# A fused attention, gated layer and routed experts: a re-costed order, an affine tie mask, single blocks for ScalarE, transposes pair by pair

## Chip, cores and metric

The kernel runs on one core of one Trainium2 chip. The metric is device microseconds of one execution; the profile has, beside it, the span from the first to the last instruction of the program.

## What is computed

Three stages follow one another: causal linear attention with decay over 2 x 8 heads of 768 positions; a layer `x @ w_in`, gated by `clip(h + 3, 0, 6) / 6`, and `@ w_out`; and a routed layer of eight experts, in which each of 1536 tokens goes to one expert and each expert takes at most 192. The third, cut:

```python
logits = x @ w_gate
order = np.argsort(-logits.flatten())
assigned, counts = -np.ones(N), np.zeros(E)
for idx in order:                       # best (token, expert) pairs first
    tok, e = int(idx) // E, int(idx) % E
    if assigned[tok] >= 0 or counts[e] >= cap:
        continue
    assigned[tok] = e
    counts[e] += 1
out = np.zeros((N, D))
for e in range(E):
    mask = assigned == e
    out[mask] = np.maximum(x[mask] @ w1[e], 0.0) @ w2[e]
```

## The kernel before

**Who sets the order.** The program is written as steps, each with an engine, a cost in us, inputs, buffers and a key. `Plan.run` (lines 95 to 160) simulates them by these numbers and emits the instructions in the order in which its simulation starts them. It picks, of the steps that could start about now on an engine, the one with the lowest key. On the chip each engine then takes its instructions in that order and waits only for real data and real buffers. So a wrong cost does not break anything; it puts instructions into another order. A PE step that depends on another engine is planned 0.16 (`LAT`) plus 0.4 (`SLACK`, line 55) after its input. Steps of SP, which issues DMAs, mostly cost 0.06 in the plan.

**Pools.** `B` has 21 buffers of 8 KB a partition, `H` 2, `Q` 11; a step that needs a buffer waits until one is free.

**Stages.** (1) Attention over twelve chunks of 128 positions (`attention`), conversion of the weights into pairs of fp16 (`weights`, `split`), and h = x @ w_in with the gate (`h_unit`). Each product is three fp16 matmuls (high by high, high by low, low by high). (2) x2 = g @ w_out (`x2_part`, lines 677 to 715), twelve blocks j of 128 tokens, 768 matmuls in all, for the last four blocks in two parts of 384 and 128 columns. In the same stretch runs the routing.

**Routing** (lines 779 to 858) takes seven phases, one after the other. In each, m holds a value per token; PE spreads it over all partitions (L787), ACT copies it to `mrow` (L789), and for each of twelve blocks i a mask G of 128 x 1536 tells which tokens come before: DVE makes blocks 0 to 7 (L816, L825), ACT makes the lower part of blocks 8 to 11 in two steps (sign, L819; step, L822), and PE counts (L838). Ties are masks `eq` per block: POOL compares blocks 0 to 5 (L795) and multiplies all six by `before`, a triangular mask, in one instruction (L797); DVE does blocks 6 to 11 in one instruction each (L801). When all counts are in, DVE makes F (L848), PE flags, DVE the next m (L762). After the last phase pos tells each token's row.

**From routing to experts.** POOL scatters xsa (three quarters of x2) and xsb (the rest and the token numbers) to DRAM, twelve scatters each (L886), issued one after the other. SP reads them back transposed for each pair of experts (L906, L907: xs), and loads row numbers (L912) and the experts' weights (L984).

**Experts.** Eight experts in four pairs. `layer1` (L931): hp = xs @ w1, a first part over xsa and a second over xsb; ACT applies relu (rr, L936); the high part of h goes to DVE (L400) and the low part to POOL (L402). `layer2` (L960): po = h @ w2, then ACT (os) and a scatter to the output. Weights come as 32 loads of 1 MB; ACT makes the high halves (L398, L393), DVE most low halves (L408).

## Time and profile before

| | us |
|---|---|
| median of 3 runs | 569.48 (568.6 to 569.69) |
| the profiled execution | 569.23 |
| its span | 567.5 |
| PE busy | 508.1 (90%) |
| DVE busy | 423.2 (75%) |
| POOL busy | 314.2 (55%) |
| ACT busy | 294.3 (52%) |

The page gives busy time per engine, a chain of work that ended last, and groups of instructions by line. A timeline merges an engine's instructions of one kind into one row: the start, the time from the first one's start to the last one's end, and in brackets the engine's idle time before them with what ended it. An instruction that is held by something it shares with another engine shows as a longer duration and not as a wait.

### The profile page before, as it was taken

The numbers are of one execution on the slowest core, as the hardware profiler recorded it, in microseconds if no ns is written. First come the engines' busy times: TensorE is split into PE (matmuls) and PEld (weight loads), VectorE is DVE, ScalarE is ACT, GpSimd is POOL, SyncE is SP. The second block draws the span as 40 slices with busy tenths as digits, with TensorE's granted clock in tenths as the row PEclk, the third lists the DMA queues.
The fourth block names the chain that finished last, engine by engine and source line by source line (L and its number), as shares of the span: only waits on it lengthen the run. The fifth ranks groups of instructions, "written<-read, shape, count | busy, mean of one in ns | idle before, by whom it ended". The sixth has DMA issues, their size and how long they took to land.

```text
span 567.5 us, 10531 instructions
## 1 busy us (share of the span) xinstructions
PE 508.1 (90%) x4293; PEld 312.1 (55%) x4295; DVE 423.2 (75%) x651; ACT 294.3 (52%) x379; POOL 314.2 (55%) x279
## 2 busy tenths in 40 slices
PE   6889789898999878999999999999556599999995
PEld 3667444587786334444444344546556268676772
DVE  6799997787989893698696897897440669989410
ACT  2137664445454545383683684585330568787510
POOL 3887596746734645164052363254882458868531
PEclk9799989898999998999999999999968799999998
DMA  7996091380148427000000003206735999995001
GB/s 231 417 413 166 19 295 58 83 253 33 43 186 183 109 43 113 1 2 1 1 1 2 1 2 117 106 9 243 274 106 83 316 383 411 348 316 243 27 20 55
DMA packets 47889, 81.02 MB, mean 143 GB/s; under 512 B 33753, under 2 KB 34785, under 8 KB 41697
## 3 DMA queue, kind: packets, MB, share of 16 engines
q1 hardware_dynamic: 45728, 73.97, 40.9%
q0 software_dynamic: 2112, 6.39, 2.9%
q8 instruction: 33, 0.54, 0.4%
q14 instruction: 16, 0.12, 0.1%
HBM read 66.61 MB, written 6.40 MB: 129 GB/s over the span
## 4 chain that ended last, share of the span: by engine, by line
PE 50%; DVE 22%; POOL 9%; issue 8%; DMA 7%; ACT 3%; SPq 0%; POOLq 0%; ACTq 0%; DVEq 0%
PE x2p L686 17%; PE hp L931 9%; PE po L960 9%; PE cp L838 3%; POOL xsa L886 3%; POOL xsb L886 2%; DVE r L576 2%; DVE G L825 2%; PE xo L541 2%; DVE wod L381 2%; PE xo L538 2%; PE h L216 1%; PE h L217 1%; DMA raw<-raw 1%; DVE wid L381 1%
## 5 line engine op out<-in xcount | busy, mean ns | idle before, releaser
L686 PE MATMUL x2p<-wo,g 128*128 128x512 f16 (+2 forms) x768 | 139.3, 327 | 2.2 <-DVE xa L701 2.0
L402 POOL TENSOR_TENSOR g<-r,g 128x512 f16<-128x512 f32 (+1 forms) x52 | 74.7, 1444 | 63.5 <-ACT g L398 63.4
L216 PE MATMUL h<-xT,wi 128*128 128x256 f16 (+2 forms) x304 | 90.4, 308 | 6.8 <-DVE r L576 6.8
L408 DVE SCALAR_TENSOR_TENSOR w<-ws,w 128x1024 f16<-128x1024 f32 x58 | 79.0, 1403 | 20.1 <-ACT w L398 20.0
L686 PEld LDWEIGHTS <-g 128*128 128x128 f16 x768 | 62.0, 98 | 57.4 <-issue 15.3
L795 POOL TENSOR_SCALAR eq<-mrow,m 128x128 bf16<-128x128 f32 x42 | 45.9, 1109 | 82.0 <-ACT mrow L789 82.0
L217 PE MATMUL h<-xT,wi 128*128 128x256 f16 (+2 forms) x304 | 90.1, 307 | 0.5 <-DVE xT L546 0.5
L218 PE MATMUL h<-xT,wi 128*128 128x256 f16 (+2 forms) x304 | 89.9, 306 | 0.0
L931 PE MATMUL hp<-xs,w 128*128 128x192 f16 x768 | 68.3, 252 | 16.3 <-DMA xs<-xsa 11.4
L931 PEld LDWEIGHTS <-w 128*128 128x128 f16 x768 | 65.7, 100 | 20.3 <-issue 18.7
L398 ACT ACTIVATE w<-ws 128x1024 f16<-128x1024 f32 x64 | 64.3, 1050 | 15.8 <-DMA ws<-w 11.2
L960 PE MATMUL po<-w,h 128*64 128x512 f16 (+1 forms) x384 | 65.8, 385 | 6.5 <-ACT rr L936 6.5
L402 POOL TENSOR_TENSOR h<-rr,h 128x384 f16<-128x384 f32 x32 | 44.5, 1396 | 36.4 <-DVE h L400 36.3
L398 ACT ACTIVATE g<-r 128x512 f16<-128x512 f32 (+1 forms) x52 | 30.5, 592 | 45.4 <-DVE r L576 45.4
L825 DVE TENSOR_SCALAR G<-mrow,m 128x1408 bf16<-128x1408 f32 (+10 forms) x77 | 52.8, 715 | 0.8 <-issue 0.8
L960 PEld LDWEIGHTS <-h 128*64 128x64 f16 (+1 forms) x384 | 29.4, 105 | 39.5 <-issue 10.0
L575 ACT ACTIVATE r<-h,c 128x512 f32<-128x512 f32 (+1 forms) x52 | 33.5, 646 | 28.9 <-PE h L218 20.2
L400 DVE TENSOR_SCALAR h<-rr 128x384 f16<-128x384 f32 x32 | 22.6, 719 | 32.3 <-ACT rr L936 32.2
L576 DVE SCALAR_TENSOR_TENSOR r<-r,h 128x512 f32<-128x512 f32 (+1 forms) x52 | 32.8, 639 | 18.2 <-ACT r L575 17.5
L819 ACT ACTIVATE G<-mrow,m 128x1536 bf16<-128x1536 f32 (+3 forms) x28 | 39.3, 1404 | 3.0 <-PE cp L838 1.7
L217 PEld LDWEIGHTS <-wi 128*128 128x128 f16 x304 | 30.2, 99 | 19.0 <-issue 7.3
L216 PEld LDWEIGHTS <-wi 128*128 128x128 f16 x304 | 30.2, 99 | 17.8 <-DVE r L576 2.8
(169 smaller groups left out, 810.9 us busy)
## 6 DMA issues: line engine op xcount, KB each, us to landing
ws<-w SPq DMA_DIRECT2D x32, 1024.0 KB, 7.4
wis<-w_in SPq DMA_DIRECT2D x8, 1024.0 KB, 14.3
wos<-w_out SPq DMA_DIRECT2D x8, 1024.0 KB, 5.9
raw<-raw SPq DMA_DIRECT2D x12, 512.0 KB, 11.8
qk<-raw SPq DMA_DIRECT2D x48, 128.0 KB, 5.1
vk<-raw SPq DMA_DIRECT2D x6, 512.0 KB, 4.4
tab<-tz SPq DMA_DIRECT2D x1, 512.0 KB, 6.3
wt<-wo SPq DMA_TRANSPOSE x16, 3.4
```

The costliest lines, as they stand in the source:

```text
L216: te.matmul(ps, lh, rh, start=start, stop=False)
L217: te.matmul(ps, lh, rl, start=False, stop=False)
L218: te.matmul(ps, ll, rh, start=False, stop=stop)
L398: h = add("se", c_se(n), lambda: se.activation(dst()[0], src(), AF.Copy, scale=sc), deps, bufs, key, reserve)
L402: lo = add("ge", c_ge(n), lambda: ge.tensor_tensor(dst()[1], src(), dst()[0], op=OP.subtract), [h], bufs, key)
L408: lo = add("ve", c_ve(n), lambda: ve.scalar_tensor_tensor(dst()[1], src(), sc, dst()[0], op0=OP.mult, op1=OP.subtract), [h], bufs, key)
L576: t = add("ve", c_ve(nf * T), lambda: ve.scalar_tensor_tensor(r[:], r[:], 6.0 * 2.0 ** -11, ps[:], op0=OP.min, op1=OP.mult), [t], [ps, r], ...
L686: te.matmul(ps[:], gsl(y, fc, j), w[:, z, fc % 4, d0:d1], start=(fc + y + z == 0), stop=(fc == 15 and y == 1))
L795: t_eq.append(add("ge", 1.06, lambda i=i, eq=eq, mrow=mrow: ge.tensor_scalar(eq[:, i], mrow[:, P * i:P * i + P], m[:, i:i + 1], None, op0= ...
L825: ve.tensor_scalar(G[:, i % 2, o:], mrow[:, o:], m[:, i:i + 1], None, op0=OP.is_le)
L931: te.matmul(ps[:, i], w[:, z, kk % 2, cl], x[:, 2 * kk + y, CAP * i0:CAP * i0 + CAP], start=(i + kk + y + z == 0), stop=(i == 1 and kk == ...
L960: te.matmul(o, h1[e][:, y, k, cl], w2[e, fh][0][:, zz, f], start=(k + y + zz == 0), stop=(k == 7 and y == 1))
```

## The change

- The plan's costs are set anew: SP steps (0.06 becomes 0.34 to 0.45 for loads, 2.3 for the four loads of a q or k part, 1.4 for a transpose of w_out, 1.25 to 4.7 for one of xs, 2.5 for the rows), the compares of DVE, the two steps of ACT, POOL's scatters and others. PE steps of the routing (keys below -1e5) get a fifth of the slack, 0.08.
- POOL's product with `before` becomes an affine selection on the same 128 x 768 elements: it keeps an element where its column is greater than its partition and writes 0 elsewhere. The ties lie in two buffers of pool Q rather than one of H.
- G of blocks 8 to 11 lies in one-block buffers of pool H rather than in pairs in B; blocks 0 to 7 stay in pairs in B.
- The transposes of pairs 1 to 3 depend, in the plan, on the first layer 1 matmuls of the pair before; in the old kernel those of xsa came after pair 0's xsb, and those of xsb after the scatters alone.
- The low part of h is made by DVE (the same line's other branch, L408) rather than by POOL.

```diff
+    URGENT = -1e5
-            t = max(t, end + (self.SAME[e] if x == e else self.LAT + self.SLACK[e]))
+            t = max(t, end + (self.SAME[e] if x == e else self.LAT + (self.SLACK[e] if s.key > self.URGENT else 0.2 * self.SLACK[e])))
...
 def c_cmp(n):
-    return 0.12 + n * 0.00058
-def c_cmp_se(n):
-    return 0.1 + n * 0.00095
+    return 0.11 + n * 0.00056
+def c_sign(n):
+    return 0.04 + n * 0.00099
+def c_step(n):
+    return 0.2 + n * 0.00073
...
-        return [add("sp", 0.06, lambda z=z: sy.dma_start(b[:, z * n:(z + 1) * n], raw_d[c, :, z * n:(z + 1) * n]),
+        return [add("sp", 0.45 if c > 3 else 0.06, lambda z=z: sy.dma_start(b[:, z * n:(z + 1) * n], raw_d[c, :, z * n:(z + 1) * n]),
...
-            ld_q = [add("sp", 0.24, lambda part=part: load(part), after, [qk], RAW_KEY[c], 0, 1 << 19) for part in (1, 0)]
+            ld_q = [add("sp", 2.3, lambda part=part: load(part), after, [qk], RAW_KEY[c], 0, 1 << 19) for part in (1, 0)]
...
-        eq = buf("H", [P, NCH, P], BF, f"eq{p}")
+        eqs = [buf("Q", [P, 6, P], BF, f"eq{p}_{i}") for i in range(2)]
...
-        t_eq = [add("ge", 0.26 * BY_GE, lambda eq=eq: ge.tensor_tensor(
-            eq[:, 0:BY_GE], eq[:, 0:BY_GE], before.unsqueeze(1).to_broadcast([P, BY_GE, P]), op=OP.mult), t_eq, [eq], GK)]
+        t_eq = [add("ge", 1.3, lambda eq=eqs[0]: ge.affine_select(
+            out=eq[:], in_=eq[:], pattern=[[0, BY_GE], [1, P]], compare_op=OP.is_gt, fill=0.0, base=0,
+            channel_multiplier=-1), t_eq, [eqs[0]], GK)]
...
-        Gs = [buf("B", [P, 2, NCH * P], BF, f"G{p}_{i}") for i in range(NCH // 2)]
+        Gs = [buf("B", [P, 2, NCH * P], BF, f"G{p}_{i}") for i in range(BY_SE // 2)]
+        Gs += [buf("H", [P, 1, NCH * P], BF, f"G{p}_{i}") for i in range(BY_SE, NCH)]
...
-                t = [add("se", c_cmp_se(o), sgn, t_row[:i // 4 + 1], [G, mrow], GK + n)]
-                t = [add("se", c_cmp_se(o), step, t, [G], GK + n)]
+                t = [add("se", c_sign(o), sgn, t_row[:i // 4 + 1], [G, mrow], GK + n)]
+                t = [add("se", c_step(o), step, t, [G], GK + n)]
...
-        first = t_xs[0][1:] if q else []
-        t_xs[q] = [add("sp", 0.06, lambda: sy.dma_start_transpose(out=xs[q][:, 0:6], in_=xsa_d[r, :]), t_sa + first, [xs[q]], key, 0, 725000),
-                   add("sp", 0.06, lambda: sy.dma_start_transpose(out=xs[q][:, 6:8], in_=xsb_d[r, 0:256]), t_sb, [xs[q]], key, 0, 242000)]
+        first = [l1_first[2 * q - 2]] if q else []
+        t_xs[q] = [add("sp", 4.7 if q else 2.4, lambda: sy.dma_start_transpose(out=xs[q][:, 0:6], in_=xsa_d[r, :]), t_sa + first, [xs[q]], key, 0, 725000),
+                   add("sp", 1.25, lambda: sy.dma_start_transpose(out=xs[q][:, 6:8], in_=xsb_d[r, 0:256]), t_sb + first, [xs[q]], key, 0, 242000)]
...
             t_h1[e] += split(lambda r=r: r[:], lambda u=u: (h1[e][:, 0, 2 * u:2 * u + 2], h1[e][:, 1, 2 * u:2 * u + 2]),
-                             384, 1.0, "ge", [t], [r, h1[e]], key - 50, "ve")
+                             384, 1.0, "ve", [t], [r, h1[e]], key - 50, "ve")
...
-    for q in range(NE // 2):
-        experts_in(q, f_key + 34 * q - 20 if q else -1e6)
-    t_rows = add("sp", 0.3, load_rows, t_sb, [], f_key, 0, 500000)
+    experts_in(0, -1e6)
+    t_rows = add("sp", 2.5, load_rows, t_sb, [], f_key, 0, 500000)
...
-                ld = add("sp", 0.06, lambda e=e, z=z, n=n, st=st, src=src: sy.dma_start(st[:], src[e, :, z * n:(z + 1) * n]),
+                ld = add("sp", 0.4, lambda e=e, z=z, n=n, st=st, src=src: sy.dma_start(st[:], src[e, :, z * n:(z + 1) * n]),
...
     for q in range(NE // 2):
+        if q:
+            experts_in(q, f_key + 34 * q - 20)
         for e in (2 * q, 2 * q + 1):
```

## Rows read from the trace of the kernel before

**Rows 1.** Stretches: bounds, length, busy (instructions) PE PEld DVE ACT POOL, clock, DMA, GB/s

```profile
0.00:236.40 236.40, 208.32 (x1795) 133.60 (x1798) 194.83 (x236) 112.14 (x163) 145.67 (x118) 0.95 0.53 159
236.40:391.00 154.60, 154.14 (x1146) 71.34 (x1144) 128.09 (x322) 97.68 (x103) 59.69 (x52) 1.00 0.12 40
391.00:417.75 26.75, 13.35 (x209) 12.17 (x206) 18.39 (x21) 11.36 (x16) 23.57 (x33) 0.87 0.62 210
417.75:448.40 30.65, 19.22 (x192) 18.42 (x192) 5.83 (x8) 5.98 (x11) 12.04 (x18) 0.83 0.58 156
448.40:561.50 113.10, 113.04 (x960) 76.56 (x959) 76.02 (x69) 66.51 (x87) 72.30 (x58) 0.98 0.64 235
```

**Rows 2.** Timeline, 384 to 450: start, us, engine, line, operation [idle before, releaser]

```profile
393.50 0.49 ACT L700 ACTIVATE xa<-x2p 128x384 f16<-128x384 f32 x1 [2.31 <-PE x2p L686]
...
398.14 8.20 PE L686 MATMUL x2p<-wo,g 128*128 128x128 f16 x144 [1.99 <-DVE xa L701]
...
408.58 0.96 POOL L886 DMA_INDIRECT xsa<-xa,pos  x1 [0.19 <-issue]
...
417.75 9.24 PE L931 MATMUL hp<-xs,w 128*128 128x192 f16 x90 [11.41 <-DMA xs<-xsa]
...
431.92 9.98 PE L931 MATMUL hp<-xs,w 128*128 128x192 f16 x102 [4.93 <-DMA xs<-xsb]
...
443.30 2.00 ACT L398 ACTIVATE w<-ws 128x1024 f16<-128x1024 f32 x2 [6.82 <-DMA ws<-w]
444.39 1.22 DVE L408 SCALAR_TENSOR_TENSOR w<-ws,w 128x1024 f16<-128x1024 f32 x1 [7.51 <-ACT w L398]
...
448.41 1.86 PE L960 MATMUL po<-w,h 128*128 128x512 f16 x4 [6.51 <-ACT rr L936]
```

**Rows 3.** Timeline of SP's queue, 430 to 454

```profile
432.82 3.90 SPq L907 DMA_TRANSPOSE xs<-xsb  x3
...
439.34 14.20 SPq L906 DMA_TRANSPOSE xs<-xsa  x3
```

**Rows 4.** Line 762, m: operation, count, min/median/max ns, first and last start

```profile
L762 DVE SCALAR_TENSOR_TENSOR m<-aprev,mx x7: 171/171/172, 260.8 to 386.7; 128x12 f32<-128x12 f32 x7
```

**Rows 5.** Timeline of one routing phase, 347 to 367

```profile
349.23 6.68 POOL L795 TENSOR_SCALAR eq<-mrow,m 128x128 bf16<-128x128 f32 x6 [11.36 <-ACT mrow L789]
...
350.14 2.65 DVE L825 TENSOR_SCALAR G<-mrow,m 128x1408 bf16<-128x1408 f32 x3
...
355.99 2.05 POOL L797 TENSOR_TENSOR eq<-eq,before 128x768 bf16<-128x768 bf16 x1
...
359.74 1.16 ACT L822 ACTIVATE G<-G 128x1152 bf16<-128x1152 bf16 x1
...
361.87 0.34 DVE L801 SCALAR_TENSOR_TENSOR eq<-mrow,m,before 128x128 bf16<-128x128 f32 x1
...
362.65 0.35 PE L838 MATMUL cp<-G,ohc 128*32 128x384 bf16 x4
```

**Rows 6.** Timeline of the same phase, 356.6 to 357.5, one instruction apart

```profile
356.46 1.99 DVE L825 TENSOR_SCALAR G<-mrow,m 128x768 bf16<-128x768 f32 x1
```

**Rows 7.** Line 797, the product: count, min/median/max ns, first and last start

```profile
L797 POOL TENSOR_TENSOR eq<-eq,before x7: 1640/2046/2052, 249.5 to 375.2; 128x768 bf16<-128x768 bf16 x7
```

**Rows 8.** Waits of DVE, 240.5 to 391: total us, times, longest

```profile
DVE F L848 <- PE cp L838: 9.4, 5, 4.1
```

**Rows 9.** Timeline of ACT, 238 to 392

```profile
274.80 1.36 ACT L819 ACTIVATE G<-mrow,m 128x1280 bf16<-128x1280 f32 x1 [1.66 <-PE cp L838]
```

**Rows 10.** Groups by line, whole span: busy us, mean ns | idle before

```profile
L701 DVE SCALAR_TENSOR_TENSOR xa<-x2p,xa 128x384 f16<-128x384 f32 x12 | 6.6, 548 | 3.4 <-ACT xb L700 3.0 <-ACT xa L700 0.4
```

**Rows 11.** Timeline of PE, 474 to 482

```profile
474.03 8.09 PE L931 MATMUL hp<-xs,w 128*128 128x192 f16 x96
```

**Rows 12.** Groups by line, 482 to 514, one pair of experts

```profile
L408 DVE SCALAR_TENSOR_TENSOR w<-ws,w 128x1024 f16<-128x1024 f32 x17 | 24.0, 1458 | 0.5 <-ACT w L398 0.5
...
L400 DVE TENSOR_SCALAR h<-rr 128x384 f16<-128x384 f32 x10 | 8.7, 874 | 1.6 <-ACT rr L936 1.6
```

## What the change does to the time: the prediction

> **What bounds the kernel now.** I read the table by stretches first, then the timeline of the stretch with the lowest shares, then its DMA queue, then one routing phase in detail. The profiled execution took 569.23 us with a span of 567.5 (1.73 lies outside); the median of the runs is 569.48. I count from 569.23 and move nothing for the 0.25.
>
> The stretches [rows 1] tell four stories. Until 236.4 (attention, weights, h) PE is busy 208.3 us and DVE 194.8: two loaded engines. From 236.4 to 391 PE is busy 154.1 of 154.6: x2 matmuls fill it, while routing runs in between. From 391 to 448.4 PE is busy 32.6 of 57.4 at a clock of 0.87 and 0.83: here time is lost. From 448.4 to 561.5 PE is busy 113.04 of 113.1: expert matmuls back to back. So 391 to 448.4 is won by ending waits, and the other stretches only by shifting them.
>
> The waits of the middle [rows 2]: PE idles 1.99 us in x2, 11.41 for the transposed xsa, 4.93 for xsb, 6.51 for ACT's rr. The first two end late because scatters cannot start before routing has given pos: PE finishes x2 at 406.3 and hp starts at 417.75. The last is an order fault: rr stands in ACT's in-order queue behind the conversion of an expert weight, which waits 6.82 for its load. And the load is late because SP issues transposes first: three of xsb in 3.90 us, then, between the weights, three of xsa in 14.20 us [rows 3].
>
> **Part 1: routing.** Last starts of m are 260.8 and 386.7 for seven phases, so six intervals of 21.0 us [rows 4]. A phase is DVE's chain of G compares, with the counts on PE behind it [rows 5].
>
> *Tie mask.* POOL's six one-input compares lie beside three DVE compares of 1408, 1280 and 1152 elements that take 2.65 together, 0.69 ns an element [rows 5]. At that rate 768 elements are 0.53, some 0.6 with a fixed part; but DVE's 768-wide compare beside POOL's product with `before` (2.05 us) takes 1.99 [rows 5, 6]. So the product holds DVE 1.4 us a phase and the one-input compares do not; the product runs seven times, 1.64 to 2.05 us each [rows 7]: up to 9.8. The affine selection has one input. No row shows one. Bounds: it holds DVE like the product (0 saved) or not at all (9.8). A loss would need a hold longer than the product's; I exclude it, one instruction of the same 768 elements. Its own length matters little: POOL ends the product at 358.04 and DVE its last tie at 362.21, so it may take 4 us longer. I take the one-input row as the nearer. ACT's last step ends at 360.90 against 362.21 [rows 5], so ACT is next after 1.3: 7 x 1.3 = 9.1.
>
> The Trainium skill, "SBUF — State Buffer", section "SBUF: two separate sides", says that the port pair which VectorE and GpSimd share is an exclusive lock that whoever starts first holds for its whole instruction, and makes no exception for a GpSimd operation with one input. The product's row agrees (1.99 for 768 elements), the one-input compares do not (2.65 for 3840). By the page the selection would save nothing; that is rival A.
>
> *PE late.* The last count starts at 362.65, 0.44 after the last tie's end [rows 5], in one of the better phases: over the seven DVE waits 9.4 us in five waits for the counts, the longest 4.1 [rows 8]. The planner had put x2 matmuls before urgent steps: 0.16 + 0.4 after their inputs, and ACT's steps were costed at 2 x 1.56 for 1536 elements. The slack for urgent steps falls to 0.08 and the second step's cost to 1.32. I give 4 of the 9.4 back to what stays late (bounds 0 and 9.4 saved): 5.4. *One-block G.* G's pairs came from pool B, and ACT waited 1.66 for a count to free one [rows 9]. ScalarE's blocks now take pool H, two buffers, used one after the other by counts that come in order; it is one source of the 9.4 and gets no gain of its own. If H were short ACT would wait again, at 1.7 per phase.
>
> So routing may end 9.1 + 5.4 = 14.5 earlier. **But PE is full there**, and that caps it: x2's work does not shrink. PE's own end of x2 cannot come before 406.3 - 2.0 = 404.3. The last xa block is out of ACT at 393.99 [rows 2]; with 0.55 for its low part on DVE [rows 10] and up to 1.3 for its turn on POOL its scatter starts by 395.8, and from the last xsa scatter (408.58) to hp (417.75) it is 9.2 [rows 2]: 405.0. hp can start at 405 to 409; I take 407.5, **-10.25** (bounds -12.75 and -1).
>
> **Part 2: the middle.** xsb scatters follow xsa's directly, and hp's first part then covers them better; of 4.93 I take **-3.5** (0 to -4.9). For the transposes: pair 1's now wait for the first matmuls of pair 0, and pairs 2 and 3 for those of pairs 1 and 2. Behind xsb of pair 0 then stand rows and weights instead of 3.90 + 14.20 us of transposes [rows 3]. With SP steps costed at 0.4 to 4.7 us instead of 0.06, ACT's order should also put rr before a weight that has not landed. Of 6.51 I take **-5** (0 to -6.5). What the move costs: each later pair's two transposes now stand between weight loads, some 14.20 / 3 = 4.7 plus 3.90 / 3 = 1.3 us of SP per pair. A pair lasts about 32 us and has eight loads, so SP has room; the weights queued behind are what waits, and PE if a half is late by over 4 us. I put 0 (bound +3).
>
> *Clock.* After the idle stretches 90 hp matmuls take 9.24 and 102 take 9.98 [rows 2]; 96 take 8.09 at full clock [rows 11], so 7.58 and 8.60: 3.0 us lost, and the 48 po after rr start low too. With the waits mostly gone I take **-3** (0 to -5).
>
> **Part 3: h's low part on DVE.** 32 POOL operations go, and 32 of 128x384 come to DVE; the same operation on xa takes 548 ns [rows 10], so 8 x 0.55 = 4.4 us a pair. In the 32 us of one pair DVE's weight halves are busy 24.0 (17 of 1458 ns) and h's high parts 8.7 (10 of 874) [rows 12]; with 4.4 more that is 37.1 and does not fit. But these prices hold POOL's two-input operations beside them, and most of those go: a weight half alone takes 1.22 [rows 2], a high part of 384 elements not over the 0.6 above. That frees 17 x 0.24 + 10 x 0.26 = 6.7: 30.4 of 32. It fits, narrowly. PE hides the lateness of a part, since po of an expert follows another expert's hp (8 us). I put 0 (-1 to +3); without the relief 5.1 a pair would show, rival E.
>
> **Part 4: the first stretch.** SP costs change the order of loads, and with it everything after c = 3. PE idles 28.1 us in 236.4 [rows 1], which truer costs may place better. No row shows the new order. Bounds: -5 and +6; I take 0, since waits can appear as easily as vanish.
>
> **Sum:** 569.23 - 10.25 - 3.5 - 5 - 3 = **547.5**.
>
> **Rivals.** *A, the selection holds DVE like the product.* The new compare costs leave no room for 1.4 us, so PE, whose urgent steps come sooner, waits up to 1.4 x 7 = 9.8 and x2 ends as late as now; hp starts 1 to 3 us earlier. Left are 3.5 + 5 + 3 and 2: 555.7. For it: the product's row; against: the compares' row.
> *B, the middle's order does not hold.* Weights land late again and ACT stays behind them, the 5 and 3 are not won: 555.5. For it: pieces wait for buffers too; against: three transposes vanish ahead of them.
> *C, the first stretch gets worse* by 6: 553.5. Nothing in the trace speaks for or against it beyond two engines near full.
> *D, slower.* With little slack in-order PE waits at every urgent step (about 15 a phase: rows, twelve counts, flags; 105 in all) and holds x2 behind each. At 0.3 us each that is 31.5: hp starts 21 us later than now, less 11.5 from the middle: 579. It turns slower from (10.25 + 11.5) / 105 = 0.21 us a step. Against it: PE does not idle there today (154.14 of 154.6), and a step planned 0.24 after its input is rarely early.
> *E, DVE bounds the pairs*: 5.1 for each of the last three, 547.5 + 15.3 = 562.8. For it: 30.4 of 32 leaves little; against: POOL's product, the hold's source, goes with it.
> *F, the order hardly differs*, within 0.2%: against it stand 7 products that are gone for certain.
>
> **Chances.** Forecast 0.53 (its own range 540 to 552), A 0.17, B 0.09, C 0.09, D 0.05, E 0.04, F 0.03. The main case, A to C and E are faster, B and C with some tail to no gain: faster by over 0.2% (about what a measurement of this kernel can tell from no change) 0.91, same 0.03, slower 0.06. The range takes in A, B, C and E, and the best sums of parts 1 and 2 (-12.75 - 4.9 - 6.5 - 5 gives 540, with -3 from the first stretch 537): 537 to 563. Under 2 in 10 is left out: D, F, and several rivals at once.
>
> **What would show it.** Part 1: no DVE compare near 2 us beside POOL's mask, no 4.1 us wait of F, intervals of m at 18 to 19 us, POOL's xsa scatters starting 10 us or more before 391, and PE still full until about 405. Part 2: one pair's transposes at a time on SP, no wait of rr behind a weight, hp's second part following the first with under 2 us between. Part 3: weight halves on DVE nearer 1.2 than 1.4 us and po without gaps. Part 4: x2 filling PE from within some 3 us of 236.4 on. It would be wrong if DVE still shows a 2 us compare per phase, if PE idles between 236 and 400, or if that stretch starts over 6 us later.

## The result, and the profile after

| | us |
|---|---|
| before, median of 4 runs beside it | 569.04 (566.05 to 569.69) |
| after, median of 4 runs | 544.47 (543.38 to 545.96) |
| ratio | 0.958, 95% interval 0.9537 to 0.9622 |
| the profiled execution of after, its span | 545.96, 544.2 |

The forecast was 547.5, with 537 to 563. Its sum was made against the profiled execution of before, 569.23; against that the profiled execution of after is 23.3 us shorter, where 21.7 were forecast.

The stretches of after, in the same columns as [rows 1]: bounds, length, busy us (instructions) of PE, PEld, DVE, ACT and POOL, granted clock, DMA share, GB/s. The first bound is that of [rows 1]; the others are after's own seams: pos, first hp, first po, last po.

```profile
0.00:236.40 236.40, 205.41 (x1694) 131.91 (x1695) 194.85 (x228) 110.07 (x161) 148.19 (x117) 0.95 0.53 159
236.40:378.60 142.20, 141.85 (x1155) 63.46 (x1152) 124.11 (x328) 94.20 (x99) 56.33 (x53) 1.00 0.13 46
378.60:409.80 31.20, 28.49 (x302) 21.33 (x300) 18.91 (x22) 13.92 (x19) 26.88 (x43) 1.00 0.50 154
409.80:426.90 17.10, 16.16 (x192) 15.87 (x192) 5.17 (x9) 5.41 (x9) 2.74 (x6) 1.00 0.77 164
426.90:538.30 111.40, 111.32 (x960) 76.17 (x959) 78.50 (x100) 69.91 (x91) 26.76 (x28) 1.00 0.74 262
```

The clock column is the first thing to see: from 236.4 on it is 1.00 (2.4 GHz) everywhere, where before had 0.87 and 0.83 from 391 to 448.4 [rows 1]. The second is PE: after 236.4 it idles 2.7 us ahead of hp, 0.9 between hp's parts, and 0.4 in all elsewhere up to the last po.

The same seams in the timeline, with the last xsa block's low part on DVE, which its scatter waits for (start, us, engine, line, operation, count, idle time before it with what ended it), to be laid beside [rows 2]:

```profile
396.93 0.56 DVE L706 SCALAR_TENSOR_TENSOR xa<-x2p,xa 128x384 f16<-128x384 f32 x1 [4.49 <-ACT xa L705]
...
401.50 0.96 POOL L894 DMA_INDIRECT xsa<-xa,pos  x1 [0.19 <-issue]
...
409.82 12.04 PE L939 MATMUL hp<-xs,w 128*128 128x192 f16 x144 [2.72 <-DMA xs<-xsa]
...
422.77 4.12 PE L939 MATMUL hp<-xs,w 128*128 128x192 f16 x48 [0.92 <-DMA xs<-xsb]
...
426.98 1.24 PE L969 MATMUL po<-w,h 128*128 128x512 f16 x5
```

hp starts 7.9 us earlier (417.75 before). From hp's start to the first po it is 17.2 us instead of 30.7: 13.5 gained. From the first po to the end of the span it is 117.2 instead of 119.1: 1.9 gained, with a clock of 1.00 instead of 0.98 up to the last po. The three sum to 23.3.

Routing, in the form of [rows 4] and [rows 7] (line, operation, count, min/median/max ns, first and last start):

```profile
L767 DVE SCALAR_TENSOR_TENSOR m<-aprev,mx x7: 172/172/173, 266.5 to 374.8; 128x12 f32<-128x12 f32 x7
L802 POOL TENSOR_SCALAR_AFFINE_SELECT eq<-eq x7: 962/963/1282, 256.8 to 365.4; 128x768 bf16<-128x768 bf16 x7
```

The waits of DVE for counts, in the form of [rows 8]:

```profile
DVE F L856 <- PE cp L846: 3.2, 6, 0.8
```

Six intervals of m take 108.3, so 18.05 us a phase instead of 21.0. The affine selection takes 0.96 us where the product took 2.05. (In the three phases of before in which no DVE compare of 768 elements was still running at its start, it took 1.64 to 1.74.) One phase of it, as a timeline, to be laid beside [rows 5] and [rows 6]:

```profile
344.56 1.24 POOL L800 TENSOR_SCALAR eq<-mrow,m 128x128 bf16<-128x128 f32 x1
344.81 0.86 DVE L833 TENSOR_SCALAR G<-mrow,m 128x1024 bf16<-128x1024 f32 x1
...
347.07 0.96 POOL L802 TENSOR_SCALAR_AFFINE_SELECT eq<-eq 128x768 bf16<-128x768 bf16 x1
347.24 1.22 DVE L824 TENSOR_SCALAR G<-mrow,m 128x768 bf16<-128x768 f32 x1
...
348.37 0.87 DVE L833 TENSOR_SCALAR G<-mrow,m 128x768 bf16<-128x768 f32 x2
```

The compare of 768 elements beside the selection takes 1.22 us and ends at 348.46, 0.43 after the selection's end at 348.03. The row below shows what 768 cost when POOL is idle: that compare and one of 256 elements take 0.87 together. So the selection does hold DVE, for its own length, and so in all seven phases: each has a compare of 768 elements beside it that takes 1.21 to 1.22. Beside the product the same compare took 1.99 [rows 6] and ended 0.41 after it (358.45 and 358.04 [rows 5, 6]). What the change saved is the shorter hold, some 0.8 us a phase, not the hold.

### The profile page after: what moved, and what is told of

It is laid out like the page before. It is cut to its first block, busy times and chain, and to the rows that moved or that the text cites. A ratio compares the mean times of both kernels' runs of the same rounds, so it can differ in the third digit from the quotient of the medians.

```text
span 544.2 us, 10512 instructions
## 1 busy us (share of the span) xinstructions
PE 503.2 (92%) x4295; PEld 308.7 (57%) x4295; DVE 421.5 (77%) x684; ACT 294.1 (54%) x379; POOL 261.8 (48%) x246
## 4 chain that ended last, share of the span: by engine, by line
PE 49%; DVE 22%; issue 10%; DMA 9%; POOL 5%; ACT 2%; SPq 2%; POOLq 0%; DVEq 0%; ACTq 0%
PE x2p L691 23%; PE hp L939 6%; PE po L969 6%; PE cp L846 4%; DVE r L581 2%; DMA ws<-w 2%; DVE wod L388 2%; POOL g L407 2%; DVE wod L379 2%; PE mp L792 2%; DVE wod L386 2%; DMA raw<-raw 1%; DVE ks L475 1%; DMA qk<-raw 1%; PE xo L546 1%
## 5 line engine op out<-in xcount | busy, mean ns | idle before, releaser
L407 POOL TENSOR_TENSOR g<-r,g 128x512 f16<-128x512 f32 (+1 forms) x52 | 79.7, 1539 | 60.2 <-ACT g L403 59.7
L221 PE MATMUL h<-xT,wi 128*128 128x256 f16 (+2 forms) x304 | 91.8, 310 | 10.1 <-DVE r L581 9.3
L222 PE MATMUL h<-xT,wi 128*128 128x256 f16 (+2 forms) x304 | 91.5, 309 | 2.1 <-DVE xT L551 2.1
L223 PE MATMUL h<-xT,wi 128*128 128x256 f16 (+2 forms) x304 | 91.5, 309 | 0.0
L800 POOL TENSOR_SCALAR eq<-mrow,m 128x128 bf16<-128x128 f32 x42 | 47.2, 1140 | 73.6 <-DVE on L773 60.7
L413 DVE SCALAR_TENSOR_TENSOR w<-ws,w 128x1024 f16<-128x1024 f32 x58 | 70.6, 1263 | 14.4 <-ACT w L403 14.4
L939 PE MATMUL hp<-xs,w 128*128 128x192 f16 x768 | 65.2, 246 | 3.6 <-DMA xs<-xsa 2.7
L939 PEld LDWEIGHTS <-w 128*128 128x128 f16 x768 | 63.2, 98 | 7.1 <-issue 5.6
L969 PE MATMUL po<-w,h 128*64 128x512 f16 (+1 forms) x384 | 64.1, 380 | 0.1
L894 POOL DMA_INDIRECT out<-os,rows x12 | 14.0, 1164 | 72.3 <-ACT os L953 72.2
L833 DVE TENSOR_SCALAR G<-mrow,m 128x1408 bf16<-128x1408 f32 (+10 forms) x77 | 48.2, 648 | 0.0
L222 PEld LDWEIGHTS <-wi 128*128 128x128 f16 x304 | 30.7, 101 | 20.4 <-issue 8.4
L221 PEld LDWEIGHTS <-wi 128*128 128x128 f16 x304 | 30.6, 101 | 19.8 <-DVE r L581 4.4
L223 PEld LDWEIGHTS <-wi 128*128 128x128 f16 x304 | 30.8, 101 | 18.1 <-issue 3.9
```

Source lines behind the costliest of these rows:

```text
L221: te.matmul(ps, lh, rh, start=start, stop=False)
L222: te.matmul(ps, lh, rl, start=False, stop=False)
L223: te.matmul(ps, ll, rh, start=False, stop=stop)
L407: lo = add("ge", c_ge(n), lambda: ge.tensor_tensor(dst()[1], src(), dst()[0], op=OP.subtract), [h], bufs, key)
L413: lo = add("ve", c_ve(n), lambda: ve.scalar_tensor_tensor(dst()[1], src(), sc, dst()[0], op0=OP.mult, op1=OP.subtract), [h], bufs, key)
L800: t_eq.append(add("ge", 1.06, lambda i=i, eq=eqs[0], mrow=mrow: ge.tensor_scalar(eq[:, i], mrow[:, P * i:P * i + P], m[:, i:i + 1], None, ...
```

## The experiments

The chips differ by a few us, so each run is read against those taken beside it, and against the ratio to the kernel before. The first four runs of the table were taken on one chip, the next four on a second, the last four on a third. Only the third has the change itself beside them (after2); on the other two the nearest runs to it are u_h, u_pairs and u_spB, each with one part undone that, as shown below, costs PE no wait. The change has a ratio of 0.958 in the result and of 0.9652 on the third chip, so ratios of different chips are not compared more finely than that, some 4 us. Seven undo one part of the change, two undo several (u_A, u_mid), one doubles a cost (d_sel), one goes beyond the change (best), and one repeats it (after2).

| run | us, median | ratio to before, interval | before there |
|---|---|---|---|
| u_tie | 547.98 | 0.9596 (0.9563 to 0.9629) | 570.8 |
| u_h | 544.40 | 0.9529 (0.9482 to 0.9576) | 570.8 |
| u_pairs | 544.86 | 0.9557 (0.9522 to 0.9591) | 570.8 |
| u_spA | 542.95 | 0.9514 (0.9481 to 0.9546) | 570.8 |
| u_A | 542.14 | 0.9527 (0.9471 to 0.9583) | 569.56 |
| d_sel | 545.98 | 0.9588 (0.9526 to 0.9649) | 569.56 |
| u_urgent | 550.63 | 0.9659 (0.9600 to 0.9717) | 569.56 |
| u_spB | 544.35 | 0.9563 (0.9501 to 0.9626) | 569.56 |
| best | 544.35 | 0.9497 (0.9468 to 0.9525) | 572.75 |
| after2 (the change again) | 552.53 | 0.9652 (0.9620 to 0.9683) | 572.75 |
| u_mid | 560.25 | 0.9791 (0.9734 to 0.9847) | 572.75 |
| u_G | 557.12 | 0.9722 (0.9686 to 0.9758) | 572.75 |

### The tie mask: the product again, and the selection twice

```diff
-        t_eq = [add("ge", 1.3, lambda eq=eqs[0]: ge.affine_select(
...
+        t_eq = [add("ge", 1.3, lambda eq=eqs[0]: ge.tensor_tensor(
+            eq[:], eq[:], before.unsqueeze(1).to_broadcast([P, BY_GE, P]), op=OP.mult), t_eq, [eqs[0]], GK)]
```

> The changed kernel with POOL's product in place of the affine selection, at the same planned cost, so that no other instruction moves. In the changed kernel a DVE compare beside the selection (0.96 us) takes 1.21 instead of 0.6; beside the product (1.64 to 2.05 us before) it took 1.99. Theory 'the mask's hold on DVE is a term of the chain': intervals of m grow from 18.0 to 18.7 to 19.0 us, pos comes 5 to 6 us later, PE waits these 0.8 us a phase at its urgent steps, and as PE is full in x2 the time grows by 2 to 6 us. Rival 'PE-bound, the hold costs nothing': pos later, time within 1 us.

In the second, the selection is done twice on the same mask:

```diff
+        def pick(eq=eqs[0]):
+            for _ in range(2):
+                ge.affine_select(out=eq[:], in_=eq[:], pattern=[[0, BY_GE], [1, P]], compare_op=OP.is_gt, ...)
...
```

> The changed kernel with the affine selection done twice in a row, at one planned cost, so that nothing else moves. If the selection holds DVE for its whole length, as the product does, one or two more DVE instructions are held: intervals of m 18.0 to 18.6 or 19.0, some 0.5 to 1.0 us a phase. If one input does not hold DVE (the forecast's reading), DVE's compares beside the second selection take their free time and m stays at 18.0 to 18.1.

Timelines of one phase, the product first, then the two selections:

```profile
350.72 1.73 POOL L802 TENSOR_TENSOR eq<-eq,before 128x768 bf16<-128x768 bf16 x1
350.88 2.00 DVE L823 TENSOR_SCALAR G<-mrow,m 128x768 bf16<-128x768 f32 x1
```

```profile
346.69 2.09 POOL L804 TENSOR_SCALAR_AFFINE_SELECT eq<-eq 128x768 bf16<-128x768 bf16 x2
346.86 1.21 DVE L826 TENSOR_SCALAR G<-mrow,m 128x768 bf16<-128x768 f32 x1
347.99 1.47 DVE L835 TENSOR_SCALAR G<-mrow,m 128x768 bf16<-128x768 f32 x2
```

With the product a phase takes 18.7 us and the time is 547.98, some 3.3 us over the two runs beside it that stand for the change (544.40 and 544.86); its fastest run, 546.67, is over their slowest, 546.20. With two selections both DVE compares are lengthened (the pair takes 1.47 where it took 0.87), a phase takes 18.5, a little under what was expected of a hold, and the time is 1.6 over the run beside it (u_spB), less than these intervals can tell apart. Both are held, each for as long as POOL's instruction lasts.

Who pays for the hold is seen in PE. The groups of PE's counts from 236 to 408, after first (u_h has the same figures), then with the product (count | busy, mean ns of one | idle before, what ended it):

```profile
L846 PE MATMUL cp<-G,ohc 128*32 128x384 bf16 x336 | 26.5, 334 | 0.0
```

```profile
L845 PE MATMUL cp<-G,ohc 128*32 128x384 bf16 x336 | 28.8, 333 | 1.9 <-DVE G L832 1.7
```

The same 336 counts take 2.3 us more, and PE idles 1.9 ahead of them: 4.2 us. x2 ends 4.5 us later than in u_h on the same chip (412.07 against 407.56), whose first m comes at the same time. With the order planned tight, PE stands at its urgent steps while DVE is held, and x2's matmuls stand behind. That is the mechanism of rival A.

### The slack of urgent steps

```diff
-    URGENT = -1e5
+    URGENT = -1e9
```

> The changed kernel with the old slack of 0.4 for urgent PE steps too. Theory 'the slack made PE late': intervals of m grow from 18.0 by 0.6 to 1.3 us (three to four hops of 0.32), pos 4 to 9 us later, and as PE is full, hp 0 to 2 us later and time 0 to 2 us longer. Rival 'the costs of the compares alone did it': intervals within 0.3 of 18.0.

m of this run, and the windows of the middle (pos to hp, hp to po):

```profile
L767 DVE SCALAR_TENSOR_TENSOR m<-aprev,mx x7: 171/171/172, 266.5 to 382.1; 128x12 f32<-128x12 f32 x7
```

```profile
386.24:411.79 25.55, 21.98 (x262) 17.41 (x260) 15.94 (x18) 9.65 (x14) 21.81 (x37) 0.98 0.56 178
411.79:432.00 20.21, 18.80 (x193) 18.19 (x193) 7.47 (x11) 7.10 (x12) 6.98 (x12) 0.86 0.94 246
```

PE and ACT there, as timelines:

```profile
411.79 18.74 PE L939 MATMUL hp<-xs,w 128*128 128x192 f16 x192 [3.57 <-DMA xs<-xsa]
431.95 10.52 PE L969 MATMUL po<-w,h 128*128 128x512 f16 x48 [1.41 <-ACT rr L945]
```

```profile
428.38 2.00 ACT L403 ACTIVATE w<-ws 128x1024 f16<-128x1024 f32 x2 [1.27 <-DMA ws<-w]
430.29 1.99 ACT L945 ACTIVATE rr<-hp 128x384 f32<-128x384 f32 x5
```

A phase takes 19.3 us instead of 18.05, so pos comes 7.6 later than in after. Of that only 2.0 reach hp's start, because x2 on PE fills the rest. But PE waits 3.57 for xsa instead of 2.72, hp to po takes 20.2 us instead of 17.1 at a clock of 0.86, and the last 1.41 of it is a wait for rr, which stands on ACT behind two weight conversions; the first of these waited 1.27 for its load. That is the order fault of the kernel before, in small. The time is 6.3 over u_spB beside it, where 0 to 2 were expected. This one constant is the largest single term of the change that these runs separate.

### Single blocks of G

```diff
-        Gs = [buf("B", [P, 2, NCH * P], BF, f"G{p}_{i}") for i in range(BY_SE // 2)]
-        Gs += [buf("H", [P, 1, NCH * P], BF, f"G{p}_{i}") for i in range(BY_SE, NCH)]
+        Gs = [buf("B", [P, 2, NCH * P], BF, f"G{p}_{i}") for i in range(NCH // 2)]
```

> The changed kernel with the masks G of ScalarE's blocks 8 to 11 again in pairs in pool B. Theory (the pairs had to wait for buffers of B early in the routing, where the first stretch still holds them; the kernel before needed 22.8 us for each of the first two phases and 21.0 for the later ones): the first two phases grow by 1 to 2.5 us, the others stay at 18.0, and since PE's x2, not the routing, sets the start of hp, the time rises by 0 to 2 us. Rival (the pool makes no difference, ACT waited for the counts and these came sooner for other reasons): all phases at 18.0, the time within 1 us.

It is to be read against after2, on the same chip. Waits in the second and third full phase of u_G, by line:

```profile
L823 DVE TENSOR_SCALAR G<-mrow,m 128x128 bf16<-128x128 f32 (+7 forms) x16 | 9.4, 600 | 0.4 <-PE cp L845 0.4
L855 DVE TENSOR_SCALAR_CACHE_REDUCE F<-cp 128x384 f16<-128x384 f32 x2 | 1.1, 558 | 2.3 <-PE cp L845 2.3
```

The intervals of m are 18.3, 19.4, 20.4 and 18.3, then 18.0: the sizes are as expected, but it is the second and the third that grow, not the first two. In them a compare waits 0.35 for a count to free its G, F waits 2.3 us for counts, and PE waits 1.84 for an x2 buffer behind DVE. u_G's last m comes 130.6 us after its first instead of 126.6, and the time is 4.6 over after2, where 0 to 2 were expected. From hp's start to the end both take 133.4 us, so all of the loss lies ahead of hp; counted from the first m, x2 ends 4.7 later, and the idle time without a cause that this chip's runs have in x2 (told below) is nearly the same in both, 6.7 and 7.0 us. Single blocks are worth something, and the forecast gave them nothing.

### The order of the first stretch

The SP costs of the loads before routing as before (u_spA), and with them the cost of an element on POOL (u_A):

```diff
-        return [add("sp", 0.45 if c > 3 else 0.06, ...   # raw; likewise w_out, q and k, vk, wt
+        return [add("sp", 0.06, ...
...
-    return 0.05 + n * 0.0023
+    return 0.05 + n * 0.00205
```

> The changed kernel with the old costs of SP steps in the first stretch alone (raw, q and k, v, w_out, transposed w_out). Theory 'these costs made routing start late, but x2 fills PE meanwhile': lq starts again near 231 instead of 238.4, pos comes 5 to 8 us earlier, hp only 0 to 4 us earlier, time 0 to 4 us shorter. Rival 'the late start is passed on whole': 6 to 8 us shorter. Second rival 'the order of the first stretch is better now in the rest': longer.

> The changed kernel with the first stretch's old costs: SP's and, with them, POOL's cost per element. Up to the first routing phase every engine's order is then that of the kernel before, and after it that of the changed kernel's rules. Theory 'the new order of the first stretch costs PE 3 us and routing 7.6': lq at 230 to 232, first m at 240 to 242, pos at 370 to 372, x2's end on PE 2 to 4 us earlier than 407.1, time 2 to 4 us shorter than the changed kernel. Rival 'routing's start is what counts': 7 us shorter. Second rival 'x2's end and not routing counts, and the rest of the order is worse': within 1 us.

In after the last matmul of wp, on which routing waits, starts at 236.6:

```profile
L631 PE MATMUL wp<-wgs,wt x64: 166/166/180, 183.1 to 236.6; 128*128 128x8 f16 x64
```

In before it ends at 228.3, and the first m comes at 240.8 instead of after's 248.3. u_spA brings the first m to 246.2, u_A to 241.7: the late start of routing is in part a matter of the first stretch's order. But in part it is not: in ten of the profiled runs DVE, ACT and POOL have after's order up to the first m, and it ends anywhere from 244.5 (after2) to 248.8 (u_h). u_spA lies inside that spread, and its pos comes 2.5 earlier than after's, where 5 to 8 were expected; u_A, best (242.8) and before lie below it. How the effect divides between SP's cost and POOL's the runs don't tell. u_A's pos comes 6.9 us earlier than after's (371.75 against 378.61); but hp only 2.55 earlier. Against u_spB on the same chip, whose first m ends 3.7 after u_A's, hp is 0.8 later, and the time is 2.2 less, which these intervals can't tell apart. The window from x2's end to hp in u_A:

```profile
399.59 0.96 POOL L894 DMA_INDIRECT xsa<-xa,pos  x1 [0.19 <-DVE w L413]
...
402.20 2.34 SPq L914 DMA_TRANSPOSE xs<-xsa  x1
...
407.27 4.95 PE L939 MATMUL hp<-xs,w 128*128 128x192 f16 x58 [3.30 <-DMA xs<-xsa]
```

PE had ended x2 at 403.97. Routing is no longer what sets hp: PE's end of x2 does, and then the last xsa scatter, whose block was ready at 394.4 and which ran 5.2 later. Eight xsb scatters stand ahead of it in the trace (the expectation of run best, below, says nine).

### The middle: pair by pair, SP's costs, h on VectorE

Each alone first. The transposes of pairs 1 to 3 where they were (u_pairs), the SP costs behind routing as they were (u_spB), the low part of h on POOL (u_h):

```diff
-        first = [l1_first[2 * q - 2]] if q else []
+        first = t_xs[0][1:] if q else []
```

> The changed kernel with the transposes of all pairs asked for early again, as before the change, but with the new costs of SP steps. Theory 'the transposes in front made the weights late': SP gives 10 us or more to transposes behind pair 0's xsb, PE waits 3 to 7 us between hp and po of pair 0, time 3 to 8 us longer. Rival 'the true costs alone cured it, since ACT's order now has rr ahead of late weights': time within 2 us.

```diff
-           add("sp", 4.7 if q else 2.4, ...   # transposes; rows 2.5, weights 0.4
+           add("sp", 0.06, ...                # rows 0.3, weights 0.06
```

> The changed kernel with the old costs of SP steps after routing (xs, rows, expert weights), its transposes still pair by pair. Theory 'true costs put ACT's rr ahead of late weights, that cured the wait': a wait of rr behind a weight returns, PE idles 3 to 7 us between hp and po of pair 0, time 3 to 8 us longer. Rival 'either of the two changes suffices': within 2 us, since early transposes with true costs cost nothing either.

```diff
-                             384, 1.0, "ve", [t], [r, h1[e]], key - 50, "ve")
+                             384, 1.0, "ge", [t], [r, h1[e]], key - 50, "ve")
```

> The changed kernel with the low part of h on POOL again. Theory 'h's low part is covered': DVE's weight halves go from 1.26 back to 1.36 to 1.4 us on the mean, PE stays full among the experts, time within 1 us. Rival 'the tail and the pairs gain from it': 2 to 4 us slower.

None of the three is slower than the change, as far as ratios of different chips tell (0.9529 to 0.9563 against 0.958), where the theories of the first two had 3 to 8 us, and in none does PE wait for rr. For u_h the groups of the experts' stretch (from 427 on) show why; first after, then u_h:

```profile
L413 DVE SCALAR_TENSOR_TENSOR w<-ws,w 128x1024 f16<-128x1024 f32 x42 | 51.8, 1279 | 6.4 <-ACT w L403 6.4
L413 DVE SCALAR_TENSOR_TENSOR h<-rr,h 128x384 f16<-128x384 f32 x29 | 16.2, 558 | 1.0
L405 DVE TENSOR_SCALAR h<-rr 128x384 f16<-128x384 f32 x28 | 12.6, 449 | 11.4 <-ACT rr L945 11.2
```

```profile
L413 DVE SCALAR_TENSOR_TENSOR w<-ws,w 128x1024 f16<-128x1024 f32 x42 | 60.3, 1475 | 6.6 <-ACT w L403 6.4
L407 POOL TENSOR_TENSOR h<-rr,h 128x384 f16<-128x384 f32 x29 | 38.1, 1320 | 17.8 <-DVE h L405 16.3 <-DMA ws<-w 1.4
L405 DVE TENSOR_SCALAR h<-rr 128x384 f16<-128x384 f32 x27 | 22.1, 828 | 8.9 <-ACT rr L945 8.7
```

With the low part on DVE, these three groups sum to 51.8 + 16.2 + 12.6 = 80.6 us; with it on POOL, DVE does less work and its two sum to 60.3 + 22.1 = 82.4. (Neighbours overlap at their ends: from 427 to 540 DVE is busy 78.4 and 80.1 us in all.) The move pays for itself on DVE, and PE, busy without a gap in both, doesn't notice.

All three undone together:

> The changed kernel with everything behind the routing as it was before: the transposes of pairs 1 to 3 in the old places (SP again issues xsb of three pairs, three weights, xsa of three pairs, then weights), the old SP costs of transposes, rows and expert weights, and the low part of h on POOL. Each of the first two alone, and the third alone, cost at most 1 us. Theory (the wait of rr behind a weight's conversion is cured by the pairwise transposes or by the SP costs, either is enough): with both undone PE idles 3 to 7 us between the first hp and the first po, and the time rises by 3 to 8 us over the changed kernel, to 548 to 552. Rival (the wait went because routing ends 12 us earlier while x2 still runs, so that weights and scatters are done before hp begins): no idle time over 1 us comes back, and the time stays within 2 us of the changed kernel.

PE and SP in u_mid, then SP in after:

```profile
417.88 16.00 PE L939 MATMUL hp<-xs,w 128*128 128x192 f16 x192
433.96 10.52 PE L969 MATMUL po<-w,h 128*128 128x512 f16 x48
445.78 4.12 PE L939 MATMUL hp<-xs,w 128*128 128x192 f16 x48 [1.30 <-DMA xs<-xsa]
...
462.31 0.42 PE L939 MATMUL hp<-xs,w 128*128 128x192 f16 x3 [2.08 <-DVE w L413]
```

```profile
427.97 4.49 SPq L915 DMA_TRANSPOSE xs<-xsb  x3
432.56 1.48 SPq L993 DMA_DIRECT2D ws<-w  x3
434.09 15.41 SPq L914 DMA_TRANSPOSE xs<-xsa  x3
```

```profile
424.43 1.74 SPq L915 DMA_TRANSPOSE xs<-xsb  x1
426.27 3.75 SPq L992 DMA_DIRECT2D ws<-w  x3
430.12 13.48 SPq L914 DMA_TRANSPOSE xs<-xsa  x1
```

The old SP order is back, transposes of three pairs in a row, and a loss comes with it: PE idles 5.7 us, and the time is 7.7 us over after2. The sizes are those of the theory (3 to 7, and 3 to 8). Its place is not: po follows hp at once, rr does not wait, and the idle time comes one pair later, 1.30 for pair 1's xsa and 4.3 in four waits for halves of pair 1's weights, whose loads stood behind SP's 15.41 us. The loss is behind hp: from hp's start to the end u_mid takes 141.4 us and after2 133.4, so it is not a matter of when hp starts. Together, then, the three parts keep pair 1's weights from being late. The runs don't tell which of them would be enough alone, as each was only taken away alone. What none of them explains is the wait for rr in pair 0, 6.5 us before: it stays away in u_mid too. It came back, as 1.41 us, in u_urgent, which has all three parts and whose routing ends 7.6 later. That speaks for the rival named before u_mid, routing's earlier end, as its cure. No run isolates it: the slack also changes the order, and in u_mid hp starts as late as in before (417.88 and 417.75), which gives the weights that much more time.

### A version beyond the change

u_A, and in the plan the xsb scatters of blocks 4 to 11 come after all xsa scatters:

```diff
-                [t_pos] + t_xb[j] + ids_in, [xbb], GK + NCH + j, 0, 2 * P * XB) for j in range(NCH)]
+                [t_pos] + t_xb[j] + ids_in + (t_sa if j > 3 else []), [xbb], GK + NCH + j, 0, 2 * P * XB) for j in range(NCH)]
```

> The changed kernel with the old costs of the first stretch's loads and the old cost of a POOL element (0.00205), and with one more dependence in the plan: the xsb scatters of blocks 4 to 11 come after all xsa scatters. In the run with those costs alone the last xsa block was in SBUF about 394.4 us from the span's start, its scatter ran at 399.6 behind nine xsb scatters, and PE waited 3.3 us for hp after x2 had ended at 404.0. Now it stands behind four. Theory (what holds hp's start is the later of PE's end of x2 and the last xsa scatter plus the transposes, and here it is the scatter's place on POOL): the last xsa scatter at 395 to 397, hp's first part 0 to 1 us behind the end of x2, so at 404 to 405 rather than 407.3; time 2 to 3.5 us below that run's 542.1, about 539. Rival: the xsb scatters, which are what is pushed back, then are late for hp's second part; PE waits there for what it gained, and the time stays at 541 to 543.

The change itself once more beside it:

> The changed kernel once more on the chip of these runs, so that the others are compared with it side by side: 543 to 546 us, 0.954 to 0.960 of the kernel before.

best takes 544.35 and after2 552.53, and their intervals to before lie apart: it beats both kernels, by 8.2 us over the change on this chip. But neither number is the one expected, 539 and 543 to 546, and the two profiled executions lie only 2.2 apart (547.57, the slowest of best's, and 549.80, the fastest of after2's), so the traces show less of the difference than the medians. In best the last xsa scatter ran at 396.25, as forecast, 0.27 after its block was ready, and hp followed x2 without a wait; x2 itself ended at 412.7 instead of 404. In after2 it ended at 414.9 instead of 407.1. PE in after2, and the windows from 395 to 406 of after, after2 and best:

```profile
396.68 0.33 PE L691 MATMUL x2p<-wo,g 128*128 128x128 f16 x3 [0.44 <-issue]
...
398.83 0.57 PE L691 MATMUL x2p<-wo,g 128*128 128x128 f16 x4 [0.99 <-issue]
...
406.11 8.80 PE L691 MATMUL x2p<-wo,g 128*128 128x128 f16 x129 [0.36 <-issue]
```

```profile
395.00:406.00 11.00, 11.00 (x185) 10.48 (x184) 6.07 (x8) 6.38 (x10) 9.47 (x17) 1.00 0.28 102
```

```profile
395.00:406.00 11.00, 4.08 (x27) 2.08 (x26) 1.95 (x2) 0.50 (x1) 8.21 (x14) 0.68 0.51 139
```

```profile
395.00:406.00 11.00, 6.94 (x77) 5.53 (x75) 1.82 (x3) 2.55 (x4) 6.74 (x14) 0.75 0.64 196
```

The same program, with the same order and with its data at hand ("issue": PE waits for nothing that the profile shows), issues 27 matmuls where it issued 185 in after: one to five at a time, 0.72 us or a multiple of it apart. It is only here, in the x2 matmuls of 128 columns, which are issued every 57 ns; and all four kernels of this chip show it, with 4.1 us (best) to 8.8 us (u_G, of which 1.84 is the wait told above) of idle time in x2, while the trace of after and those of the other two chips have no idle time of this kind there. The granted clock of after2 is 0.86 from 396 to 400 and 0.50 (1.2 GHz) from 400 to 408, behind this thin work, so what is left of x2 runs slower too. The stretch ends 1.4 to 1.9 us after the end of the last of POOL's scatters in a row, on all four. Whether it is those scatters, PE's instruction supply, or something else of this chip stays open; the records show that no data was waited for, and no run here was made to part them. Of the kernel before there is no trace from this chip; its time there is 2 to 4 us longer than elsewhere. How much of best's 8.2 us is its shorter stretch of this (3.3 us less idle time in the profiled runs) is open too, and with it what the scatters' new place is worth.

## Why the prediction was right, and where it was not

The profiled execution of after took 1.5 us less than the forecast, and that it lies so near is in part luck: hp's start gave 2.3 us less than forecast, and what lies behind it 3.9 more (13.5 and 1.9 against 11.5).

**Part 1, hp's start: -10.25 forecast, -7.9 measured.** The cap held: PE was full from 236.4 to 378.6 (141.85 of 142.20), and routing's gain went mostly into it. Step by step:

- *Tie mask, 7 x 1.3 = 9.1.* Wrong in its reason. The selection does hold DVE. The forecast took the one-input compares as the nearer row, since the DVE compares beside them were not slowed [rows 5]. The timeline above shows what that row hid: POOL's compare of 128 elements lasts 1.24 us, longer than the selection of 768 (0.96), and ends at 345.80, 0.13 after the DVE compare that runs beside it (345.67). By these rows it was POOL that was held there, and it is no single case: 29 of after's 42 POOL compares, 0.66 to 1.81 us long, end 0.14 to 0.16 after the end of a DVE compare. No run tested this direction by itself. The Trainium skill, "SBUF — State Buffer", section "SBUF: two separate sides", says that whoever starts first holds the shared pair for the whole instruction, and makes no exception for a GpSimd instruction with one input. These rows agree with it (1.22 beside 0.96, 2.00 beside 1.73), and the exception that the forecast made falls. A hold as long as the instruction is also not "nothing saved", as the forecast had read that section: the selection is the shorter one. What is saved is 0.8 us a phase by the rows, and 0.63 of the interval by u_tie: 4.4 to 5.6 instead of 9.1.
- *PE late, 5.4.* Too small. DVE's waits for counts fell from 9.4 us in five [rows 8] to 3.2 in six (shown above), and u_urgent puts the slack alone at 1.2 us a phase, 8.5 in seven.
- *One-block G, 0.* Wrong: 4.0 us over the seven phases by u_G.
- *The sum.* 14.5 was forecast; from the first m to the last it is 19.5 less (126.6 instead of 146.1). One term came out at half, two were too small, so the errors offset each other in part and the sum was still 5 short.
- *What it is worth.* Routing starts 7.5 us later than before, so pos is 12.2 earlier. x2 ends 0.75 later than before, at 407.09, and not at 404.3 as PE's own end had been put: the 2.0 us wait in x2 went, but PE idled 2.9 more in the first stretch. hp then waits 2.7 us for the last xsa scatter, which POOL had put behind xsb's. The forecast had bounded that scatter at 395.8; it ran at 401.50. Its block was ready at 397.49 instead of 394.5, and then "up to 1.3 for its turn on POOL" was the weak step: the turn took 4.0, behind four xsb scatters that were ready earlier. Run best agrees: with the later xsb scatters behind it, it ran 0.27 after its block was ready, where u_A, with the same first stretch, had 5.2.

**Part 2, the middle: -3.5, -5 and -3 forecast, 13.5 by the time from hp to po, 11.5 forecast.** xsb's wait fell by 4.0 and rr's by 6.5, both near their better bounds. The clock gave 3.1 between hp and po (192 matmuls in 16.16 instead of 19.22) and most of the 1.9 behind: 4.8 for a forecast of 3. What the forecast had wrong is the cure of rr's wait. It named the pairwise transposes and SP's costs: u_pairs and u_spB, each without one of them, have no such wait, and neither has u_mid without both; what u_mid loses it loses to pair 1's weights. The -5 came true, but its reason is not shown; u_urgent speaks for routing's earlier end, and the cause stays open. And a pair's transposes cost SP not 6.0 us: 5.63 + 1.74 for pair 1, and 13.48 + 1.34 = 14.8 for pair 2. Weight loads stood ahead of them, and PE waited for no half.

**Part 3, h on VectorE: 0, measured 0 (u_h).** The relief that was assumed is there: from u_h to after weight halves go from 1.48 to 1.28 us, high parts from 0.83 to 0.45. With 78.4 of 113 us DVE is no bound, and rival E falls.

**Part 4, the first stretch: 0 forecast within -5 and +6.** PE idles 31.0 us instead of 28.1, and routing starts 7.5 late, of which up to 4 is the spread between runs of the same order. What the old order would be worth is not clear of noise: u_A is 2.2 us under the run beside it, and its hp starts no earlier. Rival C's 6 us are not there.

**The rivals.** A was right on the hold and wrong on its size, since the selection is half as long as the product. B's late weights appear only if all three parts of the middle are undone, and then in pair 1. D did not come: with 0.08 of slack PE idles 0.3 us in the whole of after's x2, and the old slack cost 6.3. F is excluded by the ratio. Of what would show the forecast right, all came: intervals of m of 18.05, the first xsa scatter at 378.9 (12 before 391), PE full to 407, 0.92 between hp's parts, x2 from 234.0 on.

## What to carry to other kernels

A short instruction that is not slowed, beside short instructions of another engine, is no proof that the two do not exclude one another: look at the duration of both, since the one that was held may be the one on the other side. In a list schedule the costs of slack and of in-order queues can be worth more than the instructions: one constant moved 6.3 us here, and a transfer's place in POOL's queue moved that transfer by 3.3. And a loss that several changes may each prevent should be tested with all of them undone: each alone undone showed nothing here, all together 8 us.

## What was not expected of the hardware

- POOL's equality compare of 128 elements took 0.62 to 1.81 us (median 1.21) beside DVE's compares, the selection of 768 elements 0.96. As 29 of the 42 end 0.14 to 0.16 after a DVE compare, much of that time was waiting for DVE, though the profile counts it as busy.
- One transpose of xsa by SP (0.7 MB in the plan's count) held SP's queue for 13.48 us in after, while three in a row took 15.41 in u_mid and those of pairs 0 and 1 in after 2.8 and 5.6: it is not the size that sets it. What it waited for stays open.
- On one chip PE issued 128-column matmuls in groups of one to six at multiples of 0.72 us for 7 to 11 us, with nothing to wait for that the profile shows, in every kernel profiled there; in after and on the other two chips x2 ran through.
